# Retention's carried products on four 64x64 tiles, and the second weight chunk fetched and converted later

## The chip, the cores and the metric

The kernel runs on one core of one Trainium2 chip. The metric is the device time of one execution in microseconds (us), taken as the median of three runs. Times inside an execution come from a profiled execution of the same kernel and count from the start of its span.

## What is computed

The reference is a decaying attention without softmax (retention), then two feed-forward layers in fp32. The sizes are 4 batches, 8 heads, 576 positions, head dimension 64, so 2304 tokens of width 512 and a hidden width of 2048.

```python
scores = scale * np.matmul(q, k.transpose(0, 1, 3, 2))
gamma = 1.0 - 2.0 ** (-5.0 - np.arange(H, dtype=np.float32))
Dmat = np.where(rel >= 0, gamma[:, None, None] ** rel[None, :, :], 0.0)
ret = scores * Dmat[None, :, :, :]
x = np.matmul(ret, v)            # tokens x 512
h = x @ w_in;  x = (h * np.tanh(softplus(h))) @ w_out           # first layer
h = x @ w2_in; out = (h * sigmoid(1.702 * h)) @ w2_out          # second layer
```

## The kernel before

**Retention in units.** `attention()` goes through 20 units: each batch has four chunks of 128 positions ("wide" units) and one of 64 (the "rest"). Units 4, 9, 14 and 19 are rests. The decay is split into factors on v, on the mask and on the output, so that a unit needs four groups of eight small products on TensorE, one product per head:

- `scores(u)` (L875, tile `sc`): k times q for each head, with 64 rows of contraction. DVE multiplies the two resulting banks by the causal mask `cm` (L879, tile `pm`).
- `update(u)` (L898, tile `ds`): adds this unit's k times v to the running state of the batch, and `take(u)` lets ACT copy the state to SBUF (tile `state`), in two copies of 64 partitions each. A rest has no update.
- The carried products in `outputs` (L926): the state of the units before, times q. The state tile holds, for each pair of heads, a 128x128 block with the two heads' 64x64 states on its diagonal and zeros beside them, so each product contracts over 128 rows. The first unit of a batch has none.
- The own products in `outputs` (L938): `pm` times v, added in the same bank `o`. DVE multiplies the result by the output's decay and writes it to X (L956, `finish`).

On POOL, `decay_v` (L866) multiplies v of the next unit by its decay factors. PSUM has eight banks: four for `sc`, two for `ds`, two for `o`. Units are loaded by SP's DMA queue into six buffers that go round, in the order of the units.

**Weights in two parts.** The layers multiply fp32 numbers as sums of a high and a low part (F32R), with three products for each pair: high by high, high by low, low by high (`PARTS`). The first layer's weights come in 16 chunks of 128 hidden columns, each with a half 0 (of w_in) and a half 1 (of w_out). A chunk is fetched as raw words (`fetch`, L184), and `convert` makes the two parts of each half in steps that the generator yields between: a clamp on DVE (L202), two steps on ACT (`rest`, `rebase`), `sign` with a shift on DVE (L142, L214), a `join` on POOL (L218), the high part on ACT, the low part on DVE (L250). All of ACT's operations have one line, L133.

**Order.** Nothing is reordered by a scheduler: every engine does its instructions in the order in which the program issues them. Each unit and each slot of the first layer calls `position(name, step)` at fixed places, in the order "pool", "fetch", "act early", "vector", "act late"; a conversion moves on by one yielded step at the place of that name. `EARLY_AT` says for the first two chunks in which unit they are fetched and from which unit they are converted; `plan_conversion` lets every half start no earlier than planned, and half 0 of a chunk at least one step behind the half before it. The other 14 chunks follow the list `LATE`.

**The seam.** Behind unit 17 comes `up(0)`, behind unit 18 `up(1)`: the first two products of the first layer, 12 matmuls each (block 0 with 512 columns, block 1 with 256), both with chunk 0. Their results are passed through mish on ACT and split again (tile `g`; ACT's high part, DVE's low part at L457) by `elementwise(0)` in unit 18 and `elementwise(1)` in unit 19. Then `first_layer` runs over slots: slot i issues `up(i)`, `down(i - 3)`, then `elementwise(i)` and the conversions due. `up(2)` is the first with chunk 1, and `up(4)` the first with chunk 2.

Of the kernel before, what the change touches and what calls it, by code (L numbers as in the profile page):

```python
# [50 lines left out]
X_UNITS = (4, 5, 6, 7, 10, 11, 12, 13)  # L51
EARLY_AT = ((2, 8), (7, 13))
EARLY = len(EARLY_AT)
# [7 lines left out]
SPLIT = 5  # L61
LAST = 2 * NPAIR * REST + DM

# [37 lines left out]
def retention_mish_gelu_kernel(ctx: ExitStack, tc: tile.TileContext, qkv, w1, w2, first_unit, rests, out):  # L101
# [19 lines left out]

    ps = ctx.enter_context(tc.tile_pool(name="ps", bufs=1, space=PSUM))
    taken = {}

    def bank(kind, of):
        taken[kind] = taken.get(kind, -1) + 1
        return ps.tile([P, NB], F32, tag=f"b{of[taken[kind] % len(of)]}", name=kind)

# [278 lines left out]
    def up(i):  # L407
        t, m, _ = SLOTS[i]
        n = BLOCKS[t][1]

        h = hs[i] = ps.tile([P, NB], F32, tag=f"b{4 + i if i < 2 else 6 + i % 2}", name="h")
# [12 lines left out]
    def down(i, es=range(NK)):  # L424
        t, m, _ = SLOTS[i]
        n = BLOCKS[t][1]
        if begins(i):
            for e in range(NK):
                if t != SIDE:
                    acc[t, e] = ps.tile([P, NB], F32, tag=f"b{e}", name="acc")  # L430
                elif e % 2 == 0:
                    acc[t, e] = ps.tile([P, NB], F32, tag=f"b{4 + e // 2}", name="acc")
                    acc[t, e + 1] = acc[t, e][:, WIDTH:]
# [189 lines left out]
    def second_layer():  # L623
# [30 lines left out]
        def new_bank(of=None):  # L654
            if of is None:
                of = turn[0] = (turn[0] + 1) % 8
            return of, ps.tile([P, NB], F32, tag=f"b{of}", name="p")[:, :TH]

# [137 lines left out]
    def attention():  # L796
        with tc.tile_pool(name="att", bufs=1) as ap:
            loaded = {}

            def views(t, n):  # L800
                w = NPAIR * n
                return (
                    t[:, :w].rearrange("p (c s) -> p c s", c=NPAIR),
                    t[:, w : 2 * w].rearrange("p (c s) -> p c s", c=NPAIR),
                    t[:, 2 * w : 2 * w + DM],
                    t[:, 2 * w + DM : 2 * w + 2 * DM] if n == P else None,
                )
# [40 lines left out]
            load(0)  # L848
            unused = bank("unused", (3,))[:, :P]
# [4 lines left out]
            act(column[:, :1], state[0][:, 0, :1], AF.Mish)  # L854

# [4 lines left out]
            def decay_v(u):  # L860
                b, c = UNITS[u]
                n = CH[c][1]
                vv = loaded[u][2][:n].rearrange("p (h d) -> p h d", d=D)
                for eng, h, e in ((nc.vector, 0, SPLIT), (nc.gpsimd, SPLIT, H)) if u == 0 else ((nc.gpsimd, 0, H),):
                    by = vt[:n, c, h:e].unsqueeze(2).to_broadcast([n, e - h, D])
                    eng.tensor_tensor(out=vv[:, h:e], in0=vv[:, h:e], in1=by, op=ALU.mult)  # L866

            def scores(u):
                n = CH[UNITS[u][1]][1]
                qt, kt = loaded[u][:2]  # L870
                sc = [quarters(bank("sc", (0, 1, 2, 3))) for _ in range(2)]
                for p in range(NPAIR):
                    for j in range(2):
                        sl = slice(64 * j, 64 * j + 64)
                        nc.tensor.matmul(sc[j][:n, p, :n], lhsT=kt[sl, p, :], rhs=qt[sl, p, :], start=True, stop=True)  # L875
                pm[u] = []
                for j in range(2):
                    t = ap.tile([P, NPAIR, P], F32, tag="pm", name="pm", bufs=4)
                    nc.vector.tensor_tensor(  # L879
                        out=t[:n, :, :n],  # L880
                        in0=sc[j][:n, :, :n],
                        in1=cm[:n, :n].unsqueeze(1).to_broadcast([n, NPAIR, n]),
                        op=ALU.mult,
                    )
                    pm[u].append(t)

            def update(u):
# [5 lines left out]
                if c == 0:  # L893
                    sums[0] = quarters(bank("ds", (4, 5)))
                for p in range(NPAIR):
                    for j in range(2):
                        sl = slice(p * P + 64 * j, p * P + 64 * j + 64)
                        nc.tensor.matmul(  # L898
                            sums[0][64 * j : 64 * j + 64, p, :D],
                            lhsT=kk[:, sl],  # L900
                            rhs=v[:, sl],
                            start=(c == 0 and p == 0),
# [4 lines left out]
            def take(u):  # L907

                if UNITS[u][1] == NCH - 1:
                    return None  # L910
                for j in range(2):
                    sl = slice(64 * j, 64 * j + 64)
                    act(state[u % 2][sl, :, sl], sums[0][sl, :, :D])
                return state[u % 2]

            def outputs(u, before, between=lambda: None):
                c = UNITS[u][1]
                n = CH[c][1]
                qt, _, v, _ = loaded[u]
                o = quarters(bank("o", (6, 7)))  # L920


                for p in range(NPAIR if c else 0):
                    for j in range(2):
# [24 lines left out]
            def finish(u, o):  # L949
                b, c = UNITS[u]  # L950
                t0, n = CH[c]
                g0 = b * S + t0
                part = 0
                while part < n:
                    w = min(n - part, 2 * TH - (g0 + part) % (2 * TH))
                    nc.vector.tensor_tensor(  # L956
                        out=cut(slice(None), g0 + part, w),
                        in0=o[:, :, part : part + w],
                        in1=gt[:, c, :, part : part + w],
                        op=ALU.mult,  # L960
# [9 lines left out]
            for u in range(n_u):  # L970
# [71 lines left out]
    def first_layer():  # L1042
# [39 lines left out]
        def drawn(g, m, es, base):  # L1082
            def piece():
                if m == 0 and es[0] == 0:
                    for q in range(NK):
                        acc[0, q] = ps.tile([P, NB], F32, tag=f"b{q}", name="acc")
                        if q % 2 == 0:
                            acc[SIDE, q] = ps.tile([P, NB], F32, tag=f"b{4 + q // 2}", name="acc")
                            acc[SIDE, q + 1] = acc[SIDE, q][:, WIDTH:]
# [18 lines left out]
        for n_s, s in enumerate(R_ROUNDS):  # L1108
            base = two(s)[0].start
            for r in range(NR):  # L1110
# [30 lines left out]
                for n_e, p in enumerate(R_STEPS):  # L1141
                    if p == "down":
                        pieces.pop(0)()
                    elif p:
# [3 lines left out]
                        if p == 1:  # L1148
                            banks["A"] = ps.tile([P, NB], F32, tag="b6", name="p")[:, :TH]
                        elif p in (2, 7):  # L1150
                            banks["E"] = ps.tile([P, NB], F32, tag="b7", name="p")[:, :TH]
                        bank = banks["A" if p in (1, 6, 5, 3) else "E"]
# [57 lines left out]
    with tc.manual_schedule():  # L1210
        attention()
        with tc.tile_pool(name="late", bufs=1) as pool:
            late.append(pool)
# [71 lines left out]
```

## Time and profile before

| | |
|---|---|
| three runs, us | 807.82, 807.85, 807.32; median 807.82 |
| profiled execution, us | 807.84 |
| its span, us | 806.1 |
| TensorE busy | 801.2 us, 99% |
| DVE busy | 571.2 us, 71% |
| ACT busy | 442.0 us, 55% |
| POOL busy | 189.3 us, 23% |
| granted TensorE clock, share of full speed | 0.999 |
| DMA over the span | 219.68 MB, mean 273 GB/s |

Retention and up(0) and up(1) end at 70.70 us, the first layer's slots and its quartered part follow up to 452 us, then the second layer. "Busy" of TensorE is from modelled ends of pipelined matmuls. A timeline row gives a start, a length and how many instructions of one kind were merged in it; the time that a group takes on TensorE is best read from its start to the next group's start. TensorE does an fp32 product in two passes, so eight products show as x16; the layers' F32R products show as one each.

### The profile page before, as it was taken

To read this page: it belongs to the slowest core of one execution; us is meant where nothing else is said; L and a number is where in the kernel's file an instruction comes from. 1 tells how busy PE (TensorE), PEld (TensorE's weight loads), DVE (VectorE), ACT (ScalarE), POOL (GpSimd) and SP (SyncE) were. 2 spreads that over 40 slices of the span, in tenths; PEclk is the share of its full clock that TensorE was granted. 3 is DMA by queue.
4 is the path that set the end of the run, shared out by engine and by line. 5 is a ranking of instruction groups with operands and counts; after the bars stand their busy time and mean duration, and the time that the engine had idled before them with its cause. 6 is when DMAs were issued, how large, how long until landed. Compare 5 with 4: busy or idle time off the path is not lost.

```text
span 806.1 us, 14287 instructions
## 1 busy us (share of the span) xinstructions
PE 801.2 (99%) x5394; PEld 761.7 (94%) x5394; DVE 571.2 (71%) x992; ACT 442.0 (55%) x861; POOL 189.3 (23%) x251
## 2 busy tenths in 40 slices
PE   9999999999999999999999999999999999999998
PEld 8998888889999999999999999999999999999998
DVE  3897988877687676567677376798555897656775
ACT  5355867765766565666566454665233663234542
POOL 3352322220376460366570052000000000000000
PEclk9999999999999999999999999999999999999999
DMA  9994679746799895698986599888887888878884
GB/s 363 420 375 123 231 235 287 273 143 214 275 309 327 297 336 177 204 324 310 341 289 219 200 351 382 272 275 270 291 255 253 252 272 291 272 253 257 251 272 158
DMA packets 92325, 219.68 MB, mean 273 GB/s; under 512 B 6496, under 2 KB 52576, under 8 KB 90464
## 3 DMA queue, kind: packets, MB, share of 16 engines
q1 hardware_dynamic: 92112, 218.56, 80.4%
q8 instruction: 43, 0.70, 0.3%
q14 instruction: 26, 0.21, 0.1%
q10 hardware_dynamic: 144, 0.20, 0.1%
HBM read 169.98 MB, written 48.76 MB: 271 GB/s over the span
## 4 chain that ended last, share of the span: by engine, by line
PE 97%; DVE 1%; DMA 1%; ACT 0%; POOL 0%; issue 0%; SPq 0%
PE p L731 22%; PE p L682 21%; PE acc L1093 17%; PE p L1156 15%; PE h L416 8%; PE acc L437 8%; PE sc L875 2%; PE o L938 2%; PE o L926 2%; PE ds L898 1%; DMA unit<-first_unit_dram 1%; DVE cs L475 0%; DVE u L475 0%; DVE X L142 0%; ACT cs L133 0%; DVE cy L352 0%
## 5 line engine op out<-in xcount | busy, mean ns | idle before, releaser
L682 PE MATMUL p<-xop,ring 128*128 128x384 f32 x1008 | 175.6, 334 | 0.4 <-DVE cs L475 0.4
L682 PEld LDWEIGHTS p<-xop,ring 128*128 128x128 f32 x1008 | 174.7, 188 | 0.8 <-DVE cs L475 0.7
L731 PE MATMUL p<-g,ring 128*128 128x384 f32 x1008 | 175.2, 334 | 0.0
L731 PEld LDWEIGHTS p<-g,ring 128*128 128x128 f32 x1008 | 174.8, 188 | 0.0
L1093 PE MATMUL acc<-g,w 128*128 128x512 f32 (+1 forms) x768 | 143.7, 337 | 0.0
L1093 PEld LDWEIGHTS acc<-g,w 128*128 128x128 f32 x768 | 124.3, 188 | 17.1 <-DVE g L475 0.2
L1156 PE MATMUL p<-xop,ring 128*128 128x384 f32 x672 | 128.4, 337 | 0.0
L1156 PEld LDWEIGHTS p<-xop,ring 128*128 128x128 f32 x672 | 115.7, 188 | 0.3
L133 ACT ACTIVATE g<-cs 128x384 fp32r<-128x384 f32 x168 | 79.0, 517 | 60.3 <-PE p L731 60.0
L475 DVE TENSOR_TENSOR g<-cs,g 128x384 fp32r<-128x384 f32 x168 | 90.0, 554 | 26.7 <-ACT g L133 25.0
L133 ACT ACTIVATE cs<-cs 128x384 f32<-128x384 f32 x72 | 37.8, 526 | 104.7 <-DVE cs L475 104.7
L437 PE MATMUL acc<-g,w 128*128 128x512 f32 (+1 forms) x384 | 72.3, 337 | 0.0
L475 DVE TENSOR_TENSOR g<-c,g 128x384 fp32r<-128x384 f32 x64 | 44.4, 693 | 38.9 <-ACT g L133 38.5
L437 PEld LDWEIGHTS acc<-g,w 128*128 128x128 f32 x384 | 60.2, 190 | 7.6
L133 ACT ACTIVATE c<-p 128x384 f32<-128x384 f32 x64 | 31.2, 488 | 52.7 <-PE p L1156 52.5
L218 POOL TENSOR_TENSOR raw<-raw 128x512 int32<-128x512 int32 x32 | 36.5, 1141 | 96.3 <-DVE raw L214 87.0
L342 POOL TENSOR_TENSOR cy<-cy 128x128 f32<-128x128 f32 x88 | 54.3, 626 | 5.2
L475 DVE TENSOR_TENSOR cs<-cs 128x384 f32<-128x384 f32 x96 | 53.4, 556 | 0.8
L416 PE MATMUL h<-x,w 128*128 128x512 f32 x192 | 46.4, 390 | 0.0
L218 POOL TENSOR_TENSOR cy<-cr 128x256 int32<-128x256 int32 x38 | 31.2, 842 | 62.7 <-DVE cr L214 58.3
L133 ACT ACTIVATE raw<-raw 128x512 int32<-128x512 uint32 x64 | 40.6, 679 | 7.8 <-DVE raw L202 7.5
L475 DVE TENSOR_TENSOR c<-p,c 128x384 f32<-128x384 f32 x48 | 26.5, 553 | 23.9 <-ACT c L133 12.9
(94 smaller groups left out, 971.6 us busy)
## 6 DMA issues: line engine op xcount, KB each, us to landing
ring<-stream SPq DMA_DIRECT2D x168, 512.0 KB, 4.6
ring<-first_stream SPq DMA_DIRECT2D x56, 512.0 KB, 5.5
stream<-cy SPq DMA_DIRECT2D x22, 896.0 KB, 5.0
raw<-w_dram SPq DMA_DIRECT2D x32, 512.0 KB, 8.0
unit<-qkv_dram SPq DMA_DIRECT2D x14, 1024.0 KB, 13.4
cr<-w_dram SPq DMA_DIRECT2D x19, 512.0 KB, 5.7
stream<-X SPq DMA_DIRECT2D x10, 896.0 KB, 5.4
first_stream<-cy SPq DMA_DIRECT2D x16, 512.0 KB, 3.0
```

Source lines behind the costliest of these rows:

```text
L133: nc.scalar.activation(out=o, in_=i, func=f, scale=scale, bias=bias)
L218: nc.gpsimd.tensor_tensor(out=o, in0=upper, in1=bits, op=ALU.add)
L342: nc.gpsimd.tensor_tensor(out=v[:, o], in0=v[:, a], in1=v[:, b], op=op)
L416: nc.tensor.matmul(h[:, :n], lhsT=W[0, m // 2][:, m % 2, a, k * P : (k + 1) * P], rhs=xs[t, k][:, b, :n], start=((k, a, b) == order[0]), s ...
L437: nc.tensor.matmul(acc[t, e][:, :n], lhsT=W[1, m // 2][:, m % 2, a, e * P : (e + 1) * P], rhs=g[:, b, :n],  start=(begins(i) and a == 0 an ...
L475: eng.tensor_tensor(out=o, in0=a, in1=b, op=op)
L682: nc.tensor.matmul(banks[p], lhsT=w[:, k, a * P : (a + 1) * P], rhs=x[:, b, k], start=(p not in SAME and k == 0 and a == 0 and b == 0), st ...
L731: nc.tensor.matmul(banks[e, p], lhsT=w[:, e, a * P : (a + 1) * P], rhs=g[:, b], start=(p != 2 and r == 0 and a == 0 and b == 0), stop=(r = ...
L875: nc.tensor.matmul(sc[j][:n, p, :n], lhsT=kt[sl, p, :], rhs=qt[sl, p, :], start=True, stop=True)
L926: nc.tensor.matmul(o[sl, p, :n], lhsT=before[:, p, sl], rhs=qt[:, p, :], start=(p == 0), stop=True, skip_group_check=True,)
L1093: nc.tensor.matmul(acc[t, e][:, :w], lhsT=W[1, m // 2][:, m % 2, a, e * P : (e + 1) * P], rhs=g[:, b, o : o + w], start=(m == 0 and a == 0 ...
L1156: nc.tensor.matmul(bank, lhsT=w[:, a, k * P : (k + 1) * P], rhs=x[:, b, k], start=(p in (1, 2, 7) and k == 0 and a == 0 and b == 0), stop= ...
```

## The change

The products keep their number. Heads are now laid out so that heads 0 to 3 lie on partitions 0 to 63 and heads 4 to 7 on 64 to 127, and:

- The state tile holds 64x64 states only, without zeros (and without the memsets that made them). A carried product contracts over 64 rows and writes 64 partitions, so that four of them fit the array at once, in its four quarters. Row halves write to different banks: `o` is now a tile of two banks.
- ACT copies the state once, with 128 partitions.
- PSUM is divided anew for retention: three banks for `sc` in turn, one for `ds`, two times two for `o`. The later stages open their own pool behind it. h of up(0) and up(1) lies in the banks `sc1` and `ds`.
- In a rest, v is laid out on 128 partitions (64 positions by two halves of heads), its decay is one POOL operation of 128x256 for 64x512, and its scores and own products are 64x64 tiles too. A rest's load is 128x768 words in place of 128x1024.
- `update` comes between the carried and the own products in every unit; before, that was so in unit 1 only.
- The second chunk is fetched in unit 14 instead of 7, and converted from unit 17 instead of 13.

```diff
-EARLY_AT = ((2, 8), (7, 13))
+EARLY_AT = ((2, 8), (14, 17))
...
-LAST = 2 * NPAIR * REST + DM
+LAST = 2 * NPAIR * REST + DM // 2
...
-            state = [ap.tile([P, NPAIR, P], F32, name=f"state{i}") for i in range(2)]
-            nc.gpsimd.memset(state[1], 0.0)
-            nc.vector.memset(state[0], 0.0)
+            state = [ap.tile([P, NPAIR, D], F32, name=f"state{i}") for i in range(2)]
+            nc.vector.memset(column, 0.0)
...
+            def rows(r, n):
+
+                at = 64 * r if n < P else 0
+                return slice(at, at + n)
...
-                sc = [quarters(bank("sc", (0, 1, 2, 3))) for _ in range(2)]
+                sc = [quarters(ps.tile([P, NB], F32, tag=next_tag("sc", 3), name="sc")) for _ in range(2)]
...
-                        nc.tensor.matmul(sc[j][:n, p, :n], lhsT=kt[sl, p, :], rhs=qt[sl, p, :], start=True, stop=True)
+                        nc.tensor.matmul(sc[j][rows(j, n), p, :n], lhsT=kt[sl, p, :], rhs=qt[sl, p, :], start=True, stop=True)
...
-                    sums[0] = quarters(bank("ds", (4, 5)))
+                    sums[0] = quarters(ps.tile([P, NB], F32, tag="ds", name="ds"))
...
-                for j in range(2):
-                    sl = slice(64 * j, 64 * j + 64)
-                    act(state[u % 2][sl, :, sl], sums[0][sl, :, :D])
+                act(state[u % 2], sums[0][:, :, :D])
...
-                o = quarters(bank("o", (6, 7)))
-
-
-                for p in range(NPAIR if c else 0):
-                    for j in range(2):
-                        sl = slice(64 * j, 64 * j + 64)
-                        nc.tensor.matmul(
-                            o[sl, p, :n],
-                            lhsT=before[:, p, sl],
-                            rhs=qt[:, p, :],
-                            start=(p == 0),
-                            stop=True,
-                            skip_group_check=True,
-                        )
+                o = ps.tile([P, 2, NB], F32, tag=next_tag("o", 2), name="o")
+                o = o[:, :, : 2 * P].rearrange("p r (c n) -> p r c n", c=2)
+
+                def place(h):
+
+                    j = h % 2
+                    return o[64 * j : 64 * j + 64, h // 4, h // 2 % 2, :n]
+
+                for p in (0, 2) if c else ():
+                    for r in range(2):
+                        for q in (p, p + 1):
+                            sl = slice(64 * r, 64 * r + 64)
+                            nc.tensor.matmul(
+                                place(4 * r + q),
+                                lhsT=before[sl, q, :],
+                                rhs=qt[sl, q, :],
+                                start=(p == 0),
+                                stop=True,
+                                skip_group_check=True,
+                            )
                 between()
-                heads = [(p, j) for p in range(NPAIR) for j in range(2)]
-                for p, j in heads if u else sorted(heads, key=lambda h: h[1]):
-                    sl = slice(64 * j, 64 * j + 64)
+                for h in range(H) if n == P else (0, 1, 4, 5, 2, 3, 6, 7):
+                    r, p = divmod(h, NPAIR)
+                    at, q = rows(r, n), h if n == P else p
                     nc.tensor.matmul(
-                        o[sl, p, :n],
-                        lhsT=v[:n, p * P + 64 * j : p * P + 64 * j + 64],
-                        rhs=pm[u][j][:n, p, :n],
-                        start=(c == 0 and p == 0),
+                        place(h),
+                        lhsT=v[at, q * D : (q + 1) * D],
+                        rhs=pm[u][r][at, p, :n],
+                        start=(c == 0 and p < 2),
...
-                if u != 1:
-                    step_state()
-                o = outputs(u, before, *((step_state,) if u == 1 else ()))
+                o = outputs(u, before, step_state)
```

The first place is a unit on TensorE, here unit 7 and the start of unit 8 (`ds` is the state update, `o<-unit,state` the carried products, `o<-pm,unit` the own ones). Before:

```order
L898 MATMUL ds<-unit_76 64x64 x8
L926 MATMUL o<-unit_76,state_72 64x128 x8
L938 MATMUL o<-pm,unit_76 64x128 x8
L875 MATMUL sc<-rest 64x64 x8
L898 MATMUL ds<-unit_77 64x64 x8
```

and with the change:

```order
L938 MATMUL o<-unit_75,state_72 64x128 x8
L906 MATMUL ds<-unit_75 64x64 x8
L950 MATMUL o<-pm,unit_75 64x128 x8
L882 MATMUL sc<-rest 64x64 x8
L938 MATMUL o<-unit_76,state_73 64x128 x8
```

The state update stood ahead of the carried products and stands now behind them. (The rows show outputs of 64 partitions; that the carried product contracts over 64 instead of 128 rows isn't in them. All wide units with carried products read alike.)

The second place is ACT's queue from the last state copies of retention into the first slots. With the change (`raw_221` and `raw_223` are halves 0 and 1 of chunk 1, `raw_827` and `raw_829` those of chunk 2 and then, in the same tile, of chunk 3; `h_915` is up(0)'s result, `h_981` up(1)'s, `h_1056` up(2)'s; `w0` is the high part of half 0, `w8` that of half 1):

```order
L128 ACTIVATE state0_72<-ds_807 128x256
L128 ACTIVATE raw_221<-raw_221 128x512 x2
L128 ACTIVATE h_915<-h_915 128x512
L128 ACTIVATE g_974<-h_915 128x512
L128 ACTIVATE raw_223<-raw_223 128x512 x2
L128 ACTIVATE h_981<-h_981 128x256
L128 ACTIVATE g_1016<-h_981 128x256
L128 ACTIVATE w0_610<-raw_221 128x512
L128 ACTIVATE raw_827<-raw_827 128x512 x2
L128 ACTIVATE raw_829<-raw_829 128x512 x2
L128 ACTIVATE w8_660<-raw_223 128x512
L128 ACTIVATE h_1056<-h_1056 128x512
```

Before, `h` of up(0) followed straight on the last state copy, and both high parts of chunk 1 stood ahead of unit 17's state copy.

The third place is DVE's queue in the same stretch, with the change (L197 is the clamp, L137 and L209 sign and shift, L245 a low part of weights, L452 a low part of `g`, L969 the output multiply; tiles as above):

```order
L969 TENSOR_TENSOR X_60<-o_945,gt_84 128x4x128
L137 SCALAR_TENSOR_TENSOR raw_221<-raw_221 128x512
L209 TENSOR_SCALAR raw_221<-raw_221 128x512
L197 TENSOR_SCALAR raw_223<-raw_223 128x512
L969 TENSOR_TENSOR X_60<-o_995,gt_84 128x4x64
L452 TENSOR_TENSOR g_1016<-h_981,g_1016 128x256
L137 SCALAR_TENSOR_TENSOR raw_223<-raw_223 128x512
L209 TENSOR_SCALAR raw_223<-raw_223 128x512
L197 TENSOR_SCALAR raw_827<-raw_827 128x512
L197 TENSOR_SCALAR raw_829<-raw_829 128x512
L245 TENSOR_TENSOR w0_610<-raw_221,w0_610 128x512
```

The low part of chunk 1's half 0 (the last row), which up(2) reads, stands behind unit 18's and unit 19's output multiplies and two clamps of chunk 2. Before, it stood between the output multiply of unit 16 and the mask multiplies of unit 18.

## Rows read from the trace of the kernel before

**Rows 1.** The page, parts 1 (busy) and 4 (chain by engine).
```profile
PE 801.2 (99%) x5394; PEld 761.7 (94%) x5394; DVE 571.2 (71%) x992; ACT 442.0 (55%) x861; POOL 189.3 (23%) x251
...
PE 97%; DVE 1%; DMA 1%; ACT 0%; POOL 0%; issue 0%; SPq 0%
```

**Rows 2.** Stretches: busy us of each engine (instructions), granted clock, DMA share, GB/s.
```profile
36.00:64.00 28.00, 28.00 (x515) 25.19 (x512) 27.22 (x48) 13.91 (x29) 13.75 (x13) 1.00 0.81 334
...
64.88:70.70 5.82, 5.82 (x109) 5.32 (x108) 2.37 (x5) 3.22 (x7) 0.00 (x0) 1.00 0.00 0
```

**Rows 3.** TensorE's timeline around units 8 to 10: start, length, engine, line, operation.
```profile
32.97 0.69 PE L898 MATMUL ds<-unit 128*64 128x64 f32 x16
33.48 1.05 PE L926 MATMUL o<-unit,state 128*64 128x128 f32 x16
34.36 1.04 PE L938 MATMUL o<-pm,unit 128*64 128x128 f32 x16
35.33 1.16 PE L875 MATMUL sc<-unit 64*128 64x128 f32 x16
36.42 0.69 PE L926 MATMUL o<-rest,state 128*64 128x64 f32 x16
37.04 0.68 PE L938 MATMUL o<-pm,rest 64*64 64x64 f32 x16
```

**Rows 4.** TensorE's timeline at the seam: unit 18 and 19, up(2), up(3), up(4).
```profile
64.88 0.68 PE L875 MATMUL sc<-rest 64*64 64x64 f32 x16
65.49 0.69 PE L898 MATMUL ds<-unit 128*64 128x64 f32 x16
...
70.70 3.01 PE L416 MATMUL h<-x,w 128*128 128x512 f32 x12
73.56 1.60 PE L416 MATMUL h<-side,w 128*128 128x256 f32 x12
...
77.74 2.88 PE L416 MATMUL h<-x,w 128*128 128x512 f32 x12
```

**Rows 5.** ACT's timeline at the seam.
```profile
66.28 0.78 ACT L133 ACTIVATE state<-ds 64x256 f32<-64x256 f32 x2 [5.08 <-PE ds L898]
67.08 0.58 ACT L133 ACTIVATE h<-h 128x512 f32<-128x512 f32 x1
...
70.58 0.36 ACT L133 ACTIVATE h<-h 128x256 f32<-128x256 f32 x1
70.97 0.38 ACT L133 ACTIVATE g<-h 128x256 fp32r<-128x256 f32 x1
...
74.14 0.70 ACT L133 ACTIVATE w<-raw 128x512 fp32r<-128x512 f32 x1 [0.21 <-POOL raw L218]
...
75.85 2.37 ACT L133 ACTIVATE raw<-raw 128x512 int32<-128x512 uint32 x4
```

**Rows 6.** DVE's timeline at the seam.
```profile
68.33 0.69 DVE L457 TENSOR_TENSOR g<-h,g 128x512 fp32r<-128x512 f32 x1 [1.99 <-ACT g L133]
68.94 0.68 DVE L956 TENSOR_TENSOR X<-o,gt 128x512 f32<-128x512 f32 x1
...
71.73 0.68 DVE L142 SCALAR_TENSOR_TENSOR raw<-raw 128x512 int32<-128x512 int32 x1
...
81.28 1.19 DVE L250 TENSOR_TENSOR w<-raw,w 128x512 fp32r<-128x512 f32 x1
```

**Rows 7.** POOL's timeline: unit 10's decay, then joins of the conversions.
```profile
32.85 1.04 POOL L866 TENSOR_TENSOR unit<-unit,unit 128x512 f32<-128x512 f32 x1 [3.98 <-DMA unit<-qkv_dram]
...
72.96 1.15 POOL L218 TENSOR_TENSOR raw<-raw 128x512 int32<-128x512 int32 x1 [10.85 <-DVE raw L214]
...
80.77 1.15 POOL L218 TENSOR_TENSOR raw<-raw 128x512 int32<-128x512 int32 x1 [0.37 <-DVE raw L214]
```

**Rows 8.** TensorE's scores of unit 5 and DVE's mask multiplies of unit 4.
```profile
20.54 1.16 PE L875 MATMUL sc<-unit 64*128 64x128 f32 x16
...
20.64 0.75 DVE L879 TENSOR_TENSOR pm<-sc,cm 64x256 f32<-64x256 f32 x2 [1.19 <-PE sc L875]
```

More of the change, by code (lines that the diff above doesn't have):

```diff
@@ L118, in retention_mish_gelu_kernel @@
     W = {}
[L122 to L127, printed above, removed]
+    ps_now = []
     def quarters(t):
@@ L409, in up @@
         n = BLOCKS[t][1]
-        h = hs[i] = ps.tile([P, NB], F32, tag=f"b{4 + i if i < 2 else 6 + i % 2}", name="h")
+        h = hs[i] = ps_now[-1].tile([P, NB], F32, tag=f"b{6 + i % 2}" if i > 1 else ("sc1", "ds")[i], name="h")
         order = [(k, a, b) for k in range(NK) for a, b in PARTS]
@@ L656, in new_bank @@
                 of = turn[0] = (turn[0] + 1) % 8
-            return of, ps.tile([P, NB], F32, tag=f"b{of}", name="p")[:, :TH]
+            return of, ps_now[-1].tile([P, NB], F32, tag=f"b{of}", name="p")[:, :TH]
         coming = iter(())
@@ L796, in attention, with next_tag @@
     def attention():
-        with tc.tile_pool(name="att", bufs=1) as ap:
+        with tc.tile_pool(name="att", bufs=1) as ap, tc.tile_pool(name="banks", bufs=1, space=PSUM) as ps:
+            ps_now.append(ps)
+            turn = {"sc": 0, "o": 0}
+            def next_tag(kind, n):
+                tag = f"{kind}{turn[kind] % n}"
+                turn[kind] += 1
+                return tag
             loaded = {}
@@ L848, in attention @@
             load(0)
-            unused = bank("unused", (3,))[:, :P]
+            unused = ps.tile([P, 2, NB], F32, tag="o1", name="unused")[:, 0, :P]
             zeros = nc.const_aps.tensor(0.0, (P, P), F32)
@@ L852, in attention @@
                 nc.tensor.matmul(unused, lhsT=zeros, rhs=zeros, start=True, stop=True)
-            act(column[:, :1], state[0][:, 0, :1], AF.Mish)
+            act(column[:, :1], column[:, 1:2], AF.Mish)
             for u in range(1, NCH + 1):
@@ L861, in decay_v @@
                 b, c = UNITS[u]
[L862 to L865, printed above, removed]
+                vv = loaded[u][2].rearrange("p (h d) -> p h d", d=D)
+                n = vv.shape[1]
+                for eng, h, e in ((nc.vector, 0, SPLIT), (nc.gpsimd, SPLIT, H)) if u == 0 else ((nc.gpsimd, 0, n),):
+                    by = vt[:, c, h:e].unsqueeze(2).to_broadcast([P, e - h, D])
                     eng.tensor_tensor(out=vv[:, h:e], in0=vv[:, h:e], in1=by, op=ALU.mult)
+            def rows(r, n):
+                at = 64 * r if n < P else 0
+                return slice(at, at + n)
             def scores(u):
@@ L878, in scores @@
                     t = ap.tile([P, NPAIR, P], F32, tag="pm", name="pm", bufs=4)
+                    at = rows(j, n)
                     nc.vector.tensor_tensor(
-                        out=t[:n, :, :n],
-                        in0=sc[j][:n, :, :n],
-                        in1=cm[:n, :n].unsqueeze(1).to_broadcast([n, NPAIR, n]),
+                        out=t[at, :, :n],
+                        in0=sc[j][at, :, :n],
+                        in1=cm[at, at].unsqueeze(1).to_broadcast([n, NPAIR, n]),
                         op=ALU.mult,
@@ L953, in finish @@
                 part = 0
+                halves = lambda t: t.rearrange("p (r c) n -> p r c n", r=2)
                 while part < n:
@@ L956, in finish @@
                     nc.vector.tensor_tensor(
-                        out=cut(slice(None), g0 + part, w),
-                        in0=o[:, :, part : part + w],
-                        in1=gt[:, c, :, part : part + w],
+                        out=halves(cut(slice(None), g0 + part, w)),
+                        in0=o[:, :, :, part : part + w],
+                        in1=halves(gt[:, c, :, part : part + w]),
                         op=ALU.mult,
@@ L1148, in first_layer @@
                         if p == 1:
-                            banks["A"] = ps.tile([P, NB], F32, tag="b6", name="p")[:, :TH]
+                            banks["A"] = ps_now[-1].tile([P, NB], F32, tag="b6", name="p")[:, :TH]
                         elif p in (2, 7):
-                            banks["E"] = ps.tile([P, NB], F32, tag="b7", name="p")[:, :TH]
+                            banks["E"] = ps_now[-1].tile([P, NB], F32, tag="b7", name="p")[:, :TH]
                         bank = banks["A" if p in (1, 6, 5, 3) else "E"]
```

33 lines of the change are left out of this document (20 added, 13 removed).

## The prediction

> **What bounds the kernel now.** First the page: its busy table and the shares of its chain [rows 1]. TensorE is busy 801.2 of 806.1 us and 97% of the chain is its own work, so the kernel gets shorter only where TensorE issues less, and longer wherever TensorE has to wait. The profiled execution took 807.84 us around its span of 806.1; the median of the three timed runs is 807.82, so I make the sum against 807.84 and need no correction.
>
> Then the stretch tables [rows 2]. From 36 to 64 us, the middle of retention, DVE is busy 27.22 of 28 us: TensorE never waits there, but DVE has nothing to spare. From 64.88 to 70.70, the end of retention, DVE is busy 2.37 of 5.82 us and no DMA runs. The change moves work from the first stretch to the second, and the question is who waits for that work.
>
> Then TensorE's timeline for one batch of retention [rows 3], to price the products, and the timelines of TensorE, ACT, DVE and POOL at the seam between retention and the first layer [rows 4 to 7], to see what up(2), the first product with the second weight chunk, will wait for. I call A the moment at which up(0) has ended and unit 19's scores start: 64.88 us before. There up(2) starts at A + 5.8 and its third product, the first that needs a low part of the chunk, at about A + 6.3 (2 of 12 products of 2.86 us in all). In the kernel before, that chunk was converted ahead of A.
>
> **Part 1, the carried products.** Eight carried products cost 0.88 us (33.48 to 34.36) [rows 3]. Now four should run at once. No row shows such a group. Half of 0.88 is 0.44, if four really run together; 0.88 if nothing overlaps more than now. The densest group in the trace is ds with 16 passes in 0.51 us (32.97 to 33.48), 32 ns each; the new group has 16 passes too, so I take 0.51. A group followed by another tile shape costs 0.10 us more than its kind followed by the same shape: the rest's 64-column groups take 0.61 (36.42 to 37.04), where ds, with as many columns and followed by its own shape, takes 0.51. The new order puts ds between the carried and the own products, so shapes change three times a unit, not twice. The gain is 0.88 - 0.51 - 0.10 = 0.26 us per unit (unrounded), with ends 0.44 (0.44 and no price for the change of shape) and -0.10 (no overlap).
>
> The Trainium skill ("TensorE: Matmul & The Clock Gate", Part 3, packing) says that matmuls on different tiles start about 4 ns apart, so that a group of four takes hardly longer than one. By that the group would stand near the 0.44 end, and the sum below would be 0.8 us smaller; no row here shows four tiles at once.
>
> Eleven such units lie before A (u = 1, 2, 3, 6, 7, 8, 11, 12, 13, 16, 17): 2.9 us. Three rest units lose one change of shape each, as both their output groups are now 64x64: 0.3 us. Together 3.2 us.
>
> Three score banks in place of four take some back. The second score bank of a unit is now the first one of the unit before, so TensorE waits for DVE's first mask multiply. For unit 5 that is plain: its scores start at 20.54, the multiplies of unit 4 start at 20.64 and the first of the two ends near 21.0 [rows 8], a wait of about 0.5 us. Units 6 to 10, where DVE is level with TensorE, I give as much again: 1.0 us, ends 0 and 2. So A comes 2.2 us earlier.
>
> What costs nothing here: one state copy on ACT for two (0.4 us less, ACT is off the path); half the rest's decay on POOL; the memsets, done long before the first load lands; the output multiply over two banks, with as many elements. The loads lose 128 KB in each rest, and the 1 MB of the chunk leaves the queue ahead of unit 15. The tightest load I found lands at 32.85 [rows 7], 2.5 us before unit 10's scores at 35.33 [rows 3]; 1.7 us of earlier TensorE fits in that. If the cover fails, TensorE waits for loads and part of the 2.2 us goes.
>
> **Part 2, the chunk moved to units 14 and 17.** Its conversion is unchanged work (per half two short DVE steps, sign and shift, two ACT steps, a POOL join, ACT's high part, DVE's low part). The fetch moves on SP behind the last unit load and still comes many us before its first use; the DMA queue is empty after A. DVE gets back about 4 us of its busy stretch (per half 0.4 for the clamp, 1.1 for sign and shift, 0.6 for the low part), for which TensorE wasn't waiting. The price is at the seam, where every step stands in a queue. Counted from A:
>
> - ds of unit 18 ended at A + 1.3 (65.49 + 0.69) [rows 4]. It now stands behind the carried products, 0.6 later: A + 1.9. ACT copies the state from 0.1 after it, 0.4: A + 2.4.
> - ACT's two steps for half 0 (0.59 each, a quarter of 2.37 [rows 5]) come ahead of mish of up(0): A + 3.6. Mish to DVE's low part of g is 1.25 (67.08 to 68.33): A + 4.85.
> - DVE does that low part and the output multiply of unit 18 (0.6 each) [rows 6]: sign starts at A + 6.05. Sign to join is 1.23 and the join 1.18 (71.73 to 72.96 to 74.14) [rows 5, 6, 7], so half 0 is joined at A + 8.45.
> - ACT can't take it yet: ahead of it stand the two steps of half 1, which wait for a clamp that DVE issues behind sign and shift (A + 7.6), then 0.59, then mish and high part of up(1), 0.77: A + 9.0. The high part takes 0.6: A + 9.6. TensorE is there at A + 5.5. **First wait, 4.1 us.**
> - DVE: low part of g(1) from A + 9.0, sign and shift of half 1 from 9.35, two clamps of chunk 2, and the low part of half 0, which runs into POOL's join of half 1 (10.6 to 11.75). A low part beside a join took 1.19 (81.28, with the join from 80.77) [rows 6, 7], not 0.68. It ends at A + 12.3. **Second wait, 2.25 us.**
> - up(2)'s third product starts at A + 12.3, not A + 6.3: 6.0 us lost.
> - Chunk 2 is now converted one step later, both halves together. From the end of up(2) at A + 14.6 ACT does mish and high part 1.1, four steps 2.2, two high parts 1.25, mish and high part of up(3) 0.75; then DVE two low parts, 1.0: A + 21.0. TensorE gets to up(4)'s third product after up(3) and down(0) (73.56 to 77.74, 4.18) and two products, 0.45: A + 19.2. **Third wait, 1.8 us**, ends 0 and 2.5. Before it stood at 78.2, A + 13.3; now A + 21.0: 7.7 us lost in all.
>
> After up(4) the queues have the order that they had, and I take no further loss (end 2).
>
> **Sum.** 807.84 - 2.2 + 7.7 = 813.3 us, slower by 0.7%. About 0.2% (1.6 us) is what a measurement of this kernel can tell from no change.
>
> **Rivals.**
>
> 1. The clock falls in the wait. TensorE would do only two products in some 6 us. Every stretch before has the granted clock 1.00, that is 2.4 GHz, and none has such a wait, so no row speaks for or against. At 1.2 GHz the last ten products of up(2) take 4.5, not 2.27 us; what follows hides in the third wait. That gives 815.6. The Trainium skill ("TensorE: Matmul & The Clock Gate", Why this matters for your kernels) warns that an idle gap between matmul bursts sends the clock back to its lower level. By that rule the time is this rival's.
> 2. The products don't overlap in four. Then the group stays at 0.88, the extra change of shape costs 0.10 in eleven units, and A comes 1.1 us later: 807.84 + 1.1 + 7.7 = 816.6. For it: no row has four at once. Against: pairs overlap fully today.
> 3. Not slower: the retention gains more than the seam costs, which it does once A comes 7.7 us earlier. At the ends above the eleven units give 4.8 and the rests 1.0. The score group takes 1.09 us (35.33 to 36.42) [rows 3] where the own products with as many columns take 0.88 without their change of shape; if that 0.2 hides a wait for DVE which the moved conversion ends, 15 units give 3.0 more: 8.8 in all, 807.84 - 8.8 + 7.7 = 806.7. Against: the 1.09 is there in early units too, where DVE idles.
>
> **Chances.** Forecast 0.50, clock 0.25, no overlap 0.12, not slower 0.13. The last one's time lies about the edge, so I split it: faster by over 0.2% 0.07, within 0.06; the others are all slower, 0.87. The range of 809.6 to 817.2 takes in the forecast with its ends (score waits 0, 0.44 for the group, no third wait: 809.6) and rivals 1 and 2; left out are rival 3 and the ends of rivals 1 and 2.
>
> **What would show it.** Right: TensorE idle about 4 us ahead of up(2) with ACT's high part as releaser, some 2 us behind its second product with DVE's low part, and 1.8 us in up(4); up(0) ending near 62.7; a unit with carried products every 3.2 us, not 3.46; carried groups of 0.6 us with their change of shape. Wrong: no wait at up(2) (the chain from A is then misread), carried groups still at 0.88 (rival 2), a stretch after the wait with a granted clock well under 1 (rival 1), or waits of TensorE for loads around unit 10.

## The result, and the profile after

| | before | changed |
|---|---|---|
| runs, us | 807.28 to 807.85 (4) | 815.33 to 818.49 (4) |
| median, us | 807.57 | 817.40 |
| ratio, 95% interval | | 1.0119 (1.0106 to 1.0132) |
| profiled execution, us | 807.84 | 817.28 |
| its span, us | 806.1 | 815.6 |
| mean granted TensorE clock | 0.999 | 0.992 |

Slower by 1.2%: the side that was forecast (813.3), and 0.2 us above the top of the range (817.2).

First the page of the changed kernel, parts 1 (busy) and 4 (chain by engine), which answer to [rows 1]:

```profile
PE 800.3 (98%) x5394; PEld 756.0 (93%) x5394; DVE 570.7 (70%) x992; ACT 433.9 (53%) x845; POOL 187.6 (23%) x250
...
PE 93%; DVE 3%; DMA 2%; ACT 1%; issue 0%; SPq 0%; ACTq 0%
```

TensorE's busy sum is 0.9 us smaller and the span 9.5 us longer. TensorE's share of the chain fell from 97% to 93%. Next its waits (engine, operation and line, what it waited for: us in total, times, longest):

```profile
PE h L411 <- ACT w L128: 4.3, 1, 4.3
PE h L411 <- DVE w L245: 4.3, 2, 2.4
...
PE sc L882 <- DVE pm L887: 0.6, 2, 0.3
...
PE sc L882 <- DMA unit<-qkv_dram: 0.2, 1, 0.2
```

Two rows of `h` (the first layer's up products) hold 8.6 us. TensorE's timeline at the seam, against [rows 4]:

```profile
61.66 0.62 PE L882 MATMUL sc<-rest 64*64 64x64 f32 x14
...
66.11 0.41 PE L950 MATMUL o<-pm,rest 64*64 64x64 f32 x16
70.83 1.22 PE L411 MATMUL h<-x,w 128*128 128x512 f32 x2 [4.30 <-ACT w L128]
73.91 4.63 PE L411 MATMUL h<-x,w 128*128 128x512 f32 x10 [1.86 <-DVE w L245]
78.34 1.79 PE L411 MATMUL h<-side,w 128*128 128x256 f32 x12
79.97 2.91 PE L432 MATMUL acc<-g,w 128*128 128x512 f32 x12
82.74 0.73 PE L411 MATMUL h<-x,w 128*128 128x512 f32 x2
85.87 4.01 PE L411 MATMUL h<-x,w 128*128 128x512 f32 x10 [2.39 <-DVE w L245]
```

The three waits of the forecast are there: ahead of up(2), behind its second product, and behind up(4)'s second product. The last ten products of up(2) take 4.43 us to up(3)'s start, where ten of twelve took 2.38 before (73.56 - 70.70, times 10/12). The stretches (busy us of each engine, granted clock, DMA share, GB/s) say why:

```profile
63.00:70.00 7.00, 3.53 (x74) 3.08 (x70) 3.23 (x7) 4.25 (x9) 1.15 (x1) 0.90 0.00 0
70.00:76.00 6.00, 3.31 (x7) 2.20 (x8) 5.64 (x10) 3.79 (x7) 2.13 (x2) 0.50 0.90 298
76.00:80.00 4.00, 4.00 (x19) 3.41 (x19) 2.33 (x4) 1.33 (x3) 1.57 (x2) 0.65 0.90 316
80.00:84.00 4.00, 3.48 (x16) 2.34 (x14) 3.93 (x7) 3.97 (x9) 1.42 (x1) 1.00 1.06 402
84.00:90.00 6.00, 4.13 (x13) 3.34 (x14) 3.78 (x8) 2.28 (x5) 2.19 (x2) 0.72 0.15 57
```

The granted clock fell to 0.50 (1.2 GHz) while TensorE waited, came back to 1.00, and fell a second time around the wait in up(4).

What the retention itself got, in TensorE's timeline of units 9 to 12, against [rows 3]:

```profile
33.49 0.46 PE L938 MATMUL o<-rest,state 64*64 64x64 f32 x16
33.77 0.41 PE L950 MATMUL o<-pm,rest 64*64 64x64 f32 x16
34.41 1.16 PE L882 MATMUL sc<-unit 64*128 64x128 f32 x16 [0.23 <-DMA unit<-qkv_dram]
...
36.99 1.64 PE L882 MATMUL sc<-unit 64*128 64x128 f32 x16
38.56 0.67 PE L938 MATMUL o<-unit,state 64*64 64x128 f32 x16
39.16 0.69 PE L906 MATMUL ds<-unit 128*64 128x64 f32 x16
```

From start to next start, a carried group takes 0.60 us (0.88 before) and a rest's two output groups 0.28 and some 0.4 (about 0.62 each before). But unit 12's scores take 1.57, where unit 10's took 1.09 before: inside that group TensorE waits for its score bank. One load of a unit comes 0.23 us late (34.41).

### The profile page after: what moved, and what is told of

It is laid out like the page before. It is cut to its first block, busy times and chain, and to the rows that moved or that the text cites. A ratio compares the mean times of both kernels' runs of the same rounds, so it can differ in the third digit from the quotient of the medians.

```text
span 815.6 us, 14256 instructions
## 1 busy us (share of the span) xinstructions
PE 800.3 (98%) x5394; PEld 756.0 (93%) x5394; DVE 570.7 (70%) x992; ACT 433.9 (53%) x845; POOL 187.6 (23%) x250
## 4 chain that ended last, share of the span: by engine, by line
PE 93%; DVE 3%; DMA 2%; ACT 1%; issue 0%; SPq 0%; ACTq 0%
PE p L726 21%; PE p L677 20%; PE acc L1104 16%; PE p L1167 14%; PE acc L432 8%; PE h L411 8%; DMA raw<-w_dram 2%; PE sc L882 2%; PE o L950 1%; PE ds L906 1%; DVE pm L887 1%; PE o L938 1%; DMA unit<-first_unit_dram 1%; DVE X L969 0%; DVE cs L470 0%; DVE side L398 0%
## 5 line engine op out<-in xcount | busy, mean ns | idle before, releaser
L411 PE MATMUL h<-x,w 128*128 128x512 f32 x192 | 51.1, 416 | 8.6 <-ACT w L128 4.3
L411 PEld LDWEIGHTS h<-x,w 128*128 128x128 f32 x192 | 38.3, 202 | 18.3 <-DVE w L245 5.4
```

The costliest lines, as they stand in the source:

```text
L411: nc.tensor.matmul(h[:, :n], lhsT=W[0, m // 2][:, m % 2, a, k * P : (k + 1) * P], rhs=xs[t, k][:, b, :n], start=((k, a, b) == order[0]), s ...
```

## The experiments

The kernel before was run again beside each set: 807.45 us (15 runs) for the first four, 807.53 (19) for the next three, 807.46 (18) for the last two.

### The two parts, one at a time

Quarters alone:

```diff
-EARLY_AT = ((2, 8), (14, 17))
+EARLY_AT = ((2, 8), (7, 13))
```

> The changed kernel with the second chunk back in units 7 and 13, so only the four quarters are left. Theory (the quarters gain, the late conversion costs): the three waits at the seam and the low clock are gone; up(0) ends about 3 us earlier than before, perhaps 0.5 less than in the changed kernel since DVE has the conversion in units 13 to 16 again; a wait of some 0.5 us at up(2) can be new, as its bank in the new PSUM pool is one that unit 19's output multiply reads. 807.6 - 3.0 + 0.5 = 805.1 us, between 804.3 and 806. Rival (the quarters, with three score banks and a new pool, cost part of what was lost): 807.5 us or more.

Measured 806.68 us (806.47 to 808.39, 10 runs), ratio 0.9993 (0.9984 to 1.0002): 1.6 us above what was expected. A, the moment at which unit 19's scores start, is 62.54, so the retention's gain is there. But up(2) waits longer than the 0.5 us that the theory allowed, and for something else:

```profile
66.99 0.41 PE L950 MATMUL o<-pm,rest 64*64 64x64 f32 x16
69.52 2.99 PE L411 MATMUL h<-x,w 128*128 128x512 f32 x12 [2.12 <-DVE g L452]
```

up(2) waits for DVE's low part of g(1), which up(2) doesn't read. That low part reads h(1), in the bank `ds` of the attention's own PSUM pool, and up(2) writes in the pool that is opened behind it. The fifth experiment tests this. Seven of the ten runs took 806.5 to 806.8 us at a mean clock of 1.000, the other three 808.1 to 808.4 at 0.998; the profiled one is among the seven.

The moved conversion alone, in the kernel before:

```diff
-EARLY_AT = ((2, 8), (7, 13))
+EARLY_AT = ((2, 8), (14, 17))
```

> The kernel before with the second chunk in units 14 and 17, so only the late conversion. Theory: the chain from the end of up(0) is the same, so nearly the same waits open (about 4, 2 and 2.4 us) and the clock falls in them as in the changed kernel; all that is missing is the 3.2 us that retention gained: 817.4 + 3 = 820.4 us, between 819 and 822. Rival (part of the loss comes from the quarters): under 818.5 us.

Measured 818.51 us (817.81 to 820.12, 4 runs), ratio 1.0131 (1.0114 to 1.0148): under the range, at the rival's edge. The timeline has the same three waits without the quarters:

```profile
73.68 1.22 PE L416 MATMUL h<-x,w 128*128 128x512 f32 x2 [3.49 <-ACT w L133]
76.76 4.64 PE L416 MATMUL h<-x,w 128*128 128x512 f32 x10 [1.86 <-DVE w L250]
...
88.65 1.65 PE L416 MATMUL h<-x,w 128*128 128x512 f32 x4 [2.15 <-DVE w L250]
```

So the move costs 11.1 us by itself, the quarters give 0.8, and both together cost 9.8. The profiled run (820.12) is the longest of the four; the others had a mean clock of 0.996 for its 0.992. Of the four runs of the changed kernel only one has 0.996 (815.33). At equal mean clock late alone is 2.5 to 3.3 us slower than the change, near the 3 us of the theory, and the 0.8 of quarters alone is small because the wait of 2.1 us above takes most of the rest.

### The clock, with the waits left in

Products of zeros, whose result nothing reads, are put into the waits: 19 ahead of up(2), 11 behind its second product, 8 behind up(4)'s. The weights come as late as before, but TensorE doesn't stand idle.

```diff
+FILL = {"pre": 19, 2: 11, 4: 8}
...
+            nc.tensor.matmul(t[:, :P], lhsT=zeros, rhs=zeros, start=True, stop=True)
```

> The changed kernel with products of zeros (whose result nobody reads) put where TensorE waits: 19 ahead of up(2), 11 behind its second product, 8 behind up(4)'s second product, at 0.21 us each a little shorter than the waits. Theory (the waits have their length from ACT and DVE, and what comes on top is the clock): the granted clock stays 1.00, the last ten products of up(2) take 2.3 us and not 4.4, those of up(4) 2.3 and not 3.9: 817.3 - 3.7 = 813.6 us, between 812.5 and 814.5, near what was forecast without a fall of the clock. Rival (the products are slow for another reason, such as weights or banks): 817 us or more, with products as slow as in the changed kernel.

Measured 814.19 us (813.87 to 814.45, 4 runs), as expected; 3.2 us less than the changed kernel, from more work on TensorE. Its stretches and timeline:

```profile
70.00:76.00 6.00, 5.89 (x43) 5.34 (x42) 5.46 (x10) 3.99 (x7) 1.97 (x2) 1.00 0.89 289
...
84.00:90.00 6.00, 5.72 (x36) 5.24 (x37) 3.20 (x7) 2.82 (x7) 1.04 (x1) 1.00 0.21 87
```
```profile
74.16 2.55 PE L419 MATMUL h<-x,w 128*128 128x512 f32 x10
...
84.28 2.56 PE L419 MATMUL h<-x,w 128*128 128x512 f32 x10 [0.87 <-DVE w L246]
86.68 1.59 PE L440 MATMUL acc<-g,w 128*128 128x256 f32 x12
```

The clock is 1.00 in both stretches. Ten products take 2.38 us again (74.16 to 76.54), and up(4)'s third product starts at 84.28, not 85.87. So about 3.2 us of the loss is the clock, and the rest is weights that come late.

### One unit earlier

```diff
-EARLY_AT = ((2, 8), (14, 17))
+EARLY_AT = ((2, 8), (14, 16))
```

> The changed kernel with the conversion of the second chunk from unit 16 in place of 17. Theory (the place in the queues decides): half 0's clamp, sign and join each come one unit earlier and its high part is there when TensorE is, so the wait ahead of up(2) goes; its low part still stands behind unit 19's work on DVE, so a wait of 3 to 4 us moves behind the second product, and with chunk 2 a step earlier too the wait in up(4) is gone. Then 817.4 - 4.3 + 1.5 - 2.4 - 1.6 = 810.6 us if the clock falls once, 808.9 if it does not; between 808 and 811.5. Rival (the loss is that the chunk is late as a whole, in proportion): about 814 us, a quarter of the way back over four units.

Measured 810.47 us (809.74 to 810.80, 6 runs), ratio 1.0033 (1.0022 to 1.0045). The time is as expected, the place is not:

```profile
70.85 5.46 PE L411 MATMUL h<-x,w 128*128 128x512 f32 x12 [4.31 <-DVE g L452]
76.11 1.80 PE L411 MATMUL h<-side,w 128*128 128x256 f32 x12
```
```profile
70.00:76.00 6.00, 5.15 (x12) 4.12 (x13) 5.66 (x10) 2.77 (x5) 1.86 (x2) 0.50 0.91 296
```
```profile
70.62 0.68 DVE L245 TENSOR_TENSOR w<-raw,w 128x512 fp32r<-128x512 f32 x1
```

The whole wait stands ahead of up(2) and again has the low part of g(1) as releaser. Behind it the clock is 0.50 and up(2) takes 5.26 us, not 2.86. The wait in up(4) is gone. DVE does the chunk's low part right behind that of g(1), so with one pool a wait of the expected kind could stand behind up(2)'s second product; no run shows it.

### One PSUM pool

The kernel with quarters is given one pool of eight banks for its whole length, as before has it; a unit's outputs lie in two one-bank tiles. First with the early schedule:

```diff
+    ps = ctx.enter_context(tc.tile_pool(name="ps", bufs=1, space=PSUM))
+    ps_now = [ps]
...
-        with tc.tile_pool(name="att", bufs=1) as ap, tc.tile_pool(name="banks", bufs=1, space=PSUM) as ps:
+        with tc.tile_pool(name="att", bufs=1) as ap:
...
-                o = ps.tile([P, 2, NB], F32, tag=next_tag("o", 2), name="o")
+                o = [ps.tile([P, NB], F32, tag=next_tag("o", (4, 5, 0, 1)), name="o") for _ in range(2)]
...
-        ps_now.append(ctx.enter_context(tc.tile_pool(name="ps", bufs=1, space=PSUM)))
```

> Quarters with the early schedule of before (7, 13), and one pool of PSUM banks for the whole kernel, as before has it; a unit's outputs lie in two one-bank tiles, so VectorE's output multiply is two instructions. Theory (the 2.1 us that up(2) waited in quarters alone is the second PSUM pool, which opens only when the last reader of the first one, VectorE's low part of g(1), is done): that wait is gone, up(2) starts right behind the last unit's products, and the time is 806.7 - 2.1 = 804.6 us (803.9 to 805.6); the split multiplies cost VectorE some 0.1 us a unit, which may give back a few tenths in waits for score banks. Rival (up(2) waits for something else that happens to end with that low part, or the gain is taken up by a later wait of the second chunk): 806.7 (806.2 to 807.3).

Measured 805.43 us (805.06 to 805.87, 9 runs), ratio 0.9973 (0.9963 to 0.9983): 0.27% faster than the kernel before, and 1.25 us faster than quarters with two pools. The timeline shows up(2) without a wait, and a part of the gain given back at up(4):

```profile
66.91 0.41 PE L950 MATMUL o<-pm,rest 64*64 64x64 f32 x16
67.25 3.02 PE L412 MATMUL h<-x,w 128*128 128x512 f32 x12
...
74.85 3.16 PE L412 MATMUL h<-x,w 128*128 128x512 f32 x12 [0.40 <-DVE g L453]
```

up(4) writes in the bank of h(2) and waits until DVE has read that for the low part of g(2).

Then with the schedule of the change:

```diff
-EARLY_AT = ((2, 8), (7, 13))
+EARLY_AT = ((2, 8), (14, 17))
```

> The change as it stands (second chunk fetched in unit 14 and converted from unit 17), with one PSUM pool. Theory: in the change the wait for the second pool ends 0.1 us before the wait for the chunk's high part, and so is hidden behind it: 817.2 us (816 to 818.6), with the waits of 4.2, 1.9 and 2.4 us as they were. Rival (the new pool is a part of the loss, 2.1 us of it): 815.3 or less.

Measured 815.73 us (815.28 to 817.43, 4 runs), ratio 1.0105 (1.0091 to 1.0119): the median lies between the two theories. The waits are those of the theory, unchanged; the stretch of up(4) differs:

```profile
PE h L412 <- ACT w L129: 4.4, 1, 4.4
PE h L412 <- DVE w L246: 4.3, 2, 2.4
```
```profile
84.00:90.00 6.00, 4.15 (x25) 3.74 (x26) 3.77 (x8) 2.82 (x6) 2.19 (x2) 1.00 0.24 95
```

Here the clock did not fall a second time, after a wait of the same 2.4 us. Put by their mean clock, the runs of both kernels agree: at 0.996, 815.33 for the change and 815.28 to 815.79 here; at 0.991 or 0.992, 817.28 to 818.49 and 817.43. So the second pool costs the change nothing that shows, since its wait ends where the wait for the chunk's high part ends. In the two traces the second fall is the difference between 3.85 and 2.40 us for up(4)'s last ten products. That the other runs differ by some 2 us for the same reason is read from their mean clock only, and four runs of each don't tell whether the pool changes how often it comes.

### How late the conversion may be

Three more schedules of the second chunk in the kernel with one pool.

```diff
-EARLY_AT = ((2, 8), (7, 13))
+EARLY_AT = ((2, 8), (12, 14))
```

> The kernel of one pool with the second chunk fetched in unit 12 and converted from unit 14, not 7 and 13: the third chunk's place in the order stays as it was (two units before the end), so nothing behind the attention is later. Theory (what costs in a later conversion is only what is then missing at up(2)): 804.2 us (803.4 to 805.2), no more than 0.8 us faster than at (7, 13), from fewer waits for score banks in units 12 to 14. Rival (every unit that the conversion is moved back costs some 3.8 us, as from 16 to 17): 808 or more, with a wait behind up(2)'s second product.

Measured 806.66 us (806.30 to 807.45, 11 runs), ratio 0.9989 (0.9980 to 0.9998): slower than (7, 13) by 1.2, against both theories. DVE's timeline has the cause:

```profile
50.35 0.48 DVE L969 TENSOR_TENSOR X<-o,gt 128x128 f32<-128x128 f32 x2
52.38 0.43 DVE L198 TENSOR_SCALAR raw<-raw 128x512 f32<-128x512 f32 x1 [1.55 <-DMA raw<-w_dram]
52.72 1.28 DVE L887 TENSOR_TENSOR pm<-sc,cm 128x512 f32<-128x512 f32 x2
```
```profile
49.42 1.62 PE L882 MATMUL sc<-unit 64*128 64x128 f32 x16
...
52.46 0.48 PE L882 MATMUL sc<-unit 64*128 64x128 f32 x2
53.46 1.16 PE L882 MATMUL sc<-unit 64*128 64x128 f32 x14 [0.51 <-DVE pm L887]
```

The chunk had not landed when its clamp's turn came. Behind the clamp stood the mask multiplies of unit 16 (scores at 49.42), and unit 17's scores (52.46) waited for their bank. The next expectation calls these multiplies unit 17's. The 3.8 us of the rival are the way from 13 to 16 with two pools (806.68 to 810.47); from 16 to 17 it is 6.9. With the fetch in unit 9:

```diff
-EARLY_AT = ((2, 8), (12, 14))
+EARLY_AT = ((2, 8), (9, 14))
```

> The kernel of one pool with the second chunk fetched in unit 9 and converted from unit 14. In the run with (12, 14) VectorE waited 1.55 us for the chunk's transfer, in front of unit 17's mask multiplies, after units 15 and 16 had run 1.0 us ahead of the run with (7, 13). Theory (the late transfer is what cost there, and the later conversion gains): with the transfer started three units earlier that wait is gone and the time is 804.8 us (804.2 to 805.4), at or below the 805.43 of (7, 13). Rival (the conversion itself stands worse in units 14 to 17): 806 or more, with waits for score banks in unit 17.

Measured 805.45 us (805.24 to 806.26, 8 runs), ratio 0.9975 (0.9965 to 0.9985). The late transfer was the cost. Yet nothing is gained on (7, 13), though the retention ends 0.55 us earlier:

```profile
66.70 3.02 PE L412 MATMUL h<-x,w 128*128 128x512 f32 x12
...
74.88 3.17 PE L412 MATMUL h<-x,w 128*128 128x512 f32 x12 [0.99 <-DVE g L453]
```

up(4) starts at 74.88, as with (7, 13) at 74.85: the low part of g(2) sets that moment now, and what the retention gains ends there in a wait. Last, converted from unit 15:

```diff
-EARLY_AT = ((2, 8), (9, 14))
+EARLY_AT = ((2, 8), (9, 15))
```

> The same with the conversion from unit 15. Theory (a later conversion costs only what is then missing at up(2)): each of the chunk's parts is ready one unit later than with 14, the low part that up(2)'s third product needs at about 68 to 71 us, against 68.5 when it could start: 805 to 808 us, and far below the 810.5 of (14, 16). Rival (a fixed price for leaving units 13 and 14, about half of what 16 costs, whether or not up(2) waits): 808 to 810.

Measured 806.07 us (805.83 to 806.48, 11 runs), ratio 0.9981 (0.9972 to 0.9990), inside the theory's range, but not at its place. up(2) doesn't wait; up(4) does, for the low part of g(2):

```profile
75.63 3.15 PE L412 MATMUL h<-x,w 128*128 128x512 f32 x12 [1.46 <-DVE g L453]
```

From (7, 13) to (9, 15) the move costs 0.6 us, from there to (14, 17) another 9.7 (815.73): the price is what is then missing at up(2) and up(4), not a price per unit.

## Why the prediction was right on the side and too low

The prediction's markers, in us from the span's start, beside the changed kernel and the one with the waits filled, whose clock is 1.00:

| | before | predicted | changed | waits filled |
|---|---|---|---|---|
| A, unit 19's scores | 64.88 | 62.7 | 61.66 | 61.83 |
| up(2)'s third product | 71.2 | 75.0 | 73.91 | 74.16 |
| up(2) ended | 73.56 | 77.3 | 78.34 | 76.54 |
| up(4)'s third product | 78.2 | 83.7 | 85.87 | 84.28 |
| up(4) ended | 80.46 | 86.0 | 89.72 | 86.68 |
| span | 806.1 | 811.6 | 815.6 | 812.4 |

**Part 1: nearly right in its sum, wrong in two terms that cancel.** TensorE's scores of unit 1 and unit 19 start at these times, in us:

| | unit 1 | unit 19 (A) | between |
|---|---|---|---|
| before | 9.27 | 64.88 | 55.61 |
| late alone | 8.68 | 64.29 | 55.61 |
| quarters alone | 8.30 | 62.54 | 54.24 |
| changed | 8.41 | 61.66 | 53.25 |

A came 3.2 us earlier, not 2.2. But 0.9 us of this lies ahead of unit 1's scores, which had no term, and 0.6 of it is there in late alone too, which has no quarters; in the traces with quarters that start varies from 8.16 to 8.82. Between the two units the change gained 2.4 us. That this is near 2.2 is luck in part. The carried group came to 0.60 with its change of shape, 0.51 + 0.10 as taken. The Trainium skill ("TensorE: Matmul & The Clock Gate", Part 3, packing) has matmuls on different tiles start about 4 ns apart, from which the prediction estimated a group near 0.44 ahead of any change of shape; the trace has 0.60, or 0.50 without the 0.10. The rests were mis-sized: 0.3 us was forecast for three, and they gained 0.6 to 0.8 each. A rest's output groups went from 0.62 each to 0.28 and 0.4, unit 19's scores from 0.61 (64.88 to 65.49) to 0.41 (61.66 to 62.07), since all of them run on quarters now. The score banks were mis-sized the other way: 1.0 us was forecast, with ends 0 and 2. The score groups of units 5, 12, 15 and 16 alone run 0.5 to 0.8 over 1.09 each, 2.6 us together.

**Moved work: not free in the middle.** The prediction said that TensorE wasn't waiting for DVE's 4 us there. With four score banks that is so: the moved conversion alone leaves the 55.61 us between the two units as they were. With three banks it is not: the same move takes them from 54.24 to 53.25.

**Part 2: right up to up(2)'s third product, mis-sized in up(4).** The high part came at A + 9.2 (9.6 forecast), the third product at A + 12.3 (12.3). The second is right in part by luck: beside POOL's join ran the two clamps, which took longer, and not the low part behind them, which took 0.68 and not 1.19:

```profile
71.66 1.60 DVE L197 TENSOR_SCALAR raw<-raw 128x512 f32<-128x512 f32 x2
73.18 0.68 DVE L245 TENSOR_TENSOR w<-raw,w 128x512 fp32r<-128x512 f32 x1
```
```profile
71.83 1.14 POOL L213 TENSOR_TENSOR raw<-raw 128x512 int32<-128x512 int32 x1 [2.11 <-DVE raw L209]
```

At up(4) DVE's and POOL's timelines show the low part lengthened beside a join, which the prediction used at up(2) but not here:

```profile
84.29 0.41 DVE L452 TENSOR_TENSOR g<-h,g 128x256 fp32r<-128x256 f32 x1
84.62 1.79 DVE L245 TENSOR_TENSOR w<-raw,w 128x512 fp32r<-128x512 f32 x2
```
```profile
84.11 1.15 POOL L213 TENSOR_TENSOR raw<-raw 128x512 int32<-128x512 int32 x1 [0.37 <-DVE raw L209]
```

The two low parts were counted as 1.0. From the start of g(3)'s (84.29) to up(4)'s third product (85.87), which needs only the first of the chunk's two, it is 1.58. With the waits filled and the clock at 1.00 up(4)'s third product comes at A + 22.45, not A + 21.0. Of these 1.45 us the low parts are 0.6; about as much is DVE's work for a later chunk ahead of g(3)'s low part, and the rest is ACT's. As A is 0.9 earlier, the two errors partly cancel and leave 0.6 us of the miss, and the whole timeline without the clock within 0.8 us: 812.4 against 811.6.

**The step that failed is the clock.** It was rival 1, with 0.25, "what follows hides in the third wait", 815.6. The granted clock stood at 0.50 behind a wait of 4.3 us. The Trainium skill ("TensorE: Matmul & The Clock Gate", Why this matters for your kernels) warns that an idle gap between matmul bursts sends the clock back to its lower level. The trace agrees with it. The forecast put the clock at nothing, since no row of the kernel before spoke for or against it; the runs with and without zeros in the waits show 3.2 us in its place. Two things in that rival were wrong. First, the late end of up(2) does not hide. That end releases ACT's mish, and the conversion of chunk 2 stands behind it in ACT's queue; so the third wait moves along. Of the 1.8 us by which up(2) ended later than with the waits filled, 1.6 arrive at up(4)'s third product. Second, the third wait makes the clock fall again in some runs: up(4)'s last ten products took 3.85 us (85.87 to 89.72), 2.40 with the waits filled. Together 1.6 + 1.45 us; the two kernels' medians differ by 3.2.

**A term that was missing and did no harm.** The new PSUM pool holds up(2) until g(1)'s low part is done. In the change that ends at 70.68 and the high part at 70.78, so it hides; without the moved conversion it shows, 2.1 us of wait and 1.25 in the time.

**The other rivals.** Products that don't overlap (816.6) came near in time, but the carried group refutes it (its sum also leaves out the score banks and the rests, with which it is 817.3). For "not slower", A would have had to come 7.7 us earlier; it came 3.2. The terms of the range's lower end add up to 809.7, not 809.6.

## What to carry to other kernels

A conversion's price is read where its result is first needed: follow each queue from there, for the next chunk too, since what ends late releases the work behind it. Count an idle wait of several us on TensorE twice, once for the wait and once for the products behind it at the lower clock. A second memory pool is a wait on every reader of the first, and shows only when nothing later covers it: the quarters gained 2.1 us (0.9973) with one pool and the early conversion, 0.8 with two pools.

## What the runs showed of the hardware

- A group of eight 64x64 products with 64 columns, in 16 passes, took 0.28 us on four quarters, 17.5 ns a pass; the densest group before took 32 ns. With 128 columns and a change of shape the group took 0.60.
- A granted clock of 0.50 followed waits of 4.3 us (changed, one unit earlier) and of 3.5 us (late alone, 76 to 80 us). After waits of 2.1 to 2.4 us it stayed at 1.00 in two traces (quarters alone; one pool with 14, 17) and fell in two (changed, 0.72 from 84 to 90 us; late alone, 0.61 from 88.6 to 93). Products of zeros in the waits kept it at 1.00 and made the kernel 3.2 us faster.
- Beside a POOL join of 1.14 us, two clamps on DVE took 1.5 us, where one takes 0.42 otherwise (changed, 71.66). A low part took 1.19 us beside a join and 0.68 without (changed, 84.62 and 73.18).
